# Half as many spare matmuls in the waits of the first batch (75 instead of 148)

## The chip, the core and the metric

The program runs on one NeuronCore of a Trainium2 chip (trn2). The metric is the device time of one execution in microseconds (us). The engines are named as the profile names them: PE is TensorE's matmul stream and PEld its weight loads, DVE is VectorE, ACT is ScalarE, POOL is GpSimd, SP is SyncE, which here issues nearly all DMAs.

## The reference

Everything is float32. An attention with 32 memory slots per head is followed by two wide layers:

```python
def _attn_ref(q, k, v, phi):          # 8 batches, 8 heads, 576 tokens, head width 64
    a = softmax(phi over the tokens)
    k_m = einsum('bhsm,bhsd->bhmd', a, k)
    v_m = einsum('bhsm,bhsd->bhmd', a, v)
    scores = q @ k_m.T / sqrt(64)
    return softmax(scores) @ v_m
x = attention, heads side by side     # 4608 tokens x 512
h = relu(x @ w_in)                    # 2048 wide
x = (s * h * h + b) @ w_out           # 512 wide
h = x @ w1                            # 2048 wide
return (h * sigmoid(1.702 * h)) @ w2  # 512 wide
```

(Shortened; softmax stands for the exponential, the sum with 1e-9 and the division.)

## The kernel before, in words

The kernel describes its work as some thousands of small operations, each with a due time, the tiles it reads and writes and a cost for each engine that could do it. `Order.sort` (L116 on) turns them into one order for each engine by a list of costs; the program is then written out in that order, and every engine runs its own list strictly in that order. Only semaphores hold an engine up.

The work has four stages: the attention with the first layer for eight batches, then the product with `w_out`, with `w1` and with `w2`. This case plays in the first 75 us, in the first batch (b = 0), which is a chain from engine to engine:

1. `slots` (L615 on): the maximum of `phi` over the tokens (two transposes on PE, L638), the exponential (ACT, L653), then 32 small matmuls `s<-kv,ph` (L666) in two halves and 8 more (L672), which need the `kv` tiles from DMA; then the division (DVE, then ACT L688), two transposes (L638) and the copy `km` (ACT L343).
2. `beside` (L723 on): the scores (L753, tile `x`), copied by ACT (L780), transposed (L758, tile `a`), a softmax on DVE and ACT (tile `st`, last step L791), transposed back (L771, tile `y`) and split in a high and a low part, `ah` and `al` (L343, L349). It goes in two parts, 384 columns and 192 columns.
3. `matrix` (L857 on): the weights `wi`, which arrive as float64, two 32-bit words a number, and are converted by ACT, DVE and POOL (`convert`, L378 on), are multiplied by `km` (L871, tile `vw`) and split into `mh` and `ml` (L343, L881, L884).
4. `step` (L887 on): the first layer itself, twelve matmuls a tile `h` (L373 to L375), evicted as `r` (L903, L904) and stored by a DMA `r<-r`.

All inputs come in over one SP queue in a fixed order. The 41 first issues load `phi`, `kv`, `q` and the sixteen `wi` tiles of this batch and the `phi` and `kv` of the next. Behind them stand, in this order, the first store `r<-r`, the next batch's last `kv`, the two scalars `moe_s` and `moe_b` (each broadcast to 128 partitions) and so on; the first tile of `w_out` (`raw<-in_wo`) is the 61st issue. ACT converts that tile (L400) just ahead of the second batch's `km` (L343), which PE needs for that batch's scores (`a<-q,km`, L717).

In the waits of the first batch PE is given spare matmuls: 128 columns of the identity times the identity into a PSUM tile that the next real matmul clears. How many stands in the table `SPARE`, keyed by the tile that the real work opens; `sort` puts the number ahead of the PE operation, and the first use of the tile writes that many. A spare matmul is float32, and PE makes two passes for it, so the trace shows two records for each:

```python
out.append(lambda n=self.SPARE.get(self.opens[n], 0): self.fill and self.fill(n))
...
def idle(self, x, g):
    for _ in range(self.spare):
        self.nc.tensor.matmul(x[:, g, 0:P], self.ident, self.ident, start=True, stop=True)
    self.spare = 0
```

Ten more spare matmuls (`warm`, L1515 on) open the program; they are not in the table.

Of the kernel before, what the change touches and what calls it, by code (L numbers as in the profile page):

```python
# [27 lines left out]
class Order:  # L28
# [7 lines left out]

    SPARE = {
        (('ps', ('s', 0, 0)),): 12,
        (('ps', ('s', 0, 2)),): 15,
        (('ps', ('s', 0, 2)), ('ps', ('s', 0, 2), 1)): 29,  # L40
        (('ps', ('s', 0, 3)),): 10,
        (('ps', ('x', 0, 0)),): 13,
        (('ps', ('vw', 0, 0)),): 8,
        (('ps', ('y', 0, 0)),): 26,
        (('ps', ('h', 0, 0, 0)),): 19,
        (('ps', ('y', 0, 1)),): 4,
        (('ps', ('h', 0, 0, 1)),): 7,
        (('ps', ('s', 1, 0)),): 5,
    }
    FILL, AHEAD, SLACK = 2.5, 120, 0.3  # L50

# [1620 lines left out]
```

## Time and profile before

| what | us |
|---|---|
| median of 3 executions | 1353.36 (1353.16 to 1353.96) |
| the profiled execution | 1354.47 |
| its span, from the first to the last instruction | 1352.7 |
| PE busy in the span | 1344.5 (99%), 9260 passes |
| DVE busy | 1151.1 (85%) |
| ACT busy | 871.4 (64%) |
| POOL busy | 114.8 (8%) |

The profiled execution is 1.1 us above the median and 1.8 us longer than its span. A busy share says how long an engine had an instruction in it, spare matmuls included, so PE's 99% says nothing of what the work was for. The trace can be asked for the instructions of a stretch in order of time, for the waits, for the chain of work that ended last and for the DMAs with the time from their issue to their landing.

### The profile page before, as it was taken

How to read it: one execution, taken by the hardware profiler on the slowest of the kernel's cores; microseconds unless marked ns; L12 is line 12 of the kernel's file. 1: busy time of each engine (PE TensorE's matmuls, PEld its weight loads, DVE VectorE, ACT ScalarE, POOL GpSimd, SP SyncE). 2: the span in 40 equal slices, each digit the busy share in tenths (PEclk: the TensorE clock that was granted, in tenths of full speed). 3: DMA queues.
4: the chain of work that ended last, by engine and by line, in shares of the span. 5: the costliest groups of instructions: out<-in, count | busy, mean ns of one | idle time of the engine just before them, and what ended most of it. 6: DMA issues, size and time to landing. Idle time of an engine off the chain costs nothing.

```text
span 1352.7 us, 24676 instructions
## 1 busy us (share of the span) xinstructions
PE 1344.5 (99%) x9260; PEld 1304.3 (96%) x9260; DVE 1151.1 (85%) x1715; ACT 871.4 (64%) x1230; POOL 114.8 (8%) x112
## 2 busy tenths in 40 slices
PE   9999999999999999999999999999999999999998
PEld 8988888889999999999999999999999999999998
DVE  4778898899999999999998889696375979989995
ACT  3666666698778887898775666565353544645543
POOL 1211231210001000100100000000000001101011
PEclk9999999999999999999999999999999999999999
DMA  9689999897787695898799799879599969779884
GB/s 370 229 307 331 330 354 352 315 339 262 271 270 211 181 311 173 234 320 288 213 343 352 276 360 362 320 270 337 190 372 388 317 204 248 193 235 234 278 245 93
DMA packets 155961, 381.33 MB, mean 282 GB/s; under 512 B 17344, under 2 KB 30528, under 8 KB 155840
## 3 DMA queue, kind: packets, MB, share of 16 engines
q1 hardware_dynamic: 146048, 362.23, 74.8%
q0 software_dynamic: 9792, 17.50, 8.8%
q8 instruction: 73, 1.20, 0.4%
q14 instruction: 48, 0.39, 0.1%
HBM read 226.12 MB, written 153.55 MB: 281 GB/s over the span
## 4 chain that ended last, share of the span: by engine, by line
PE 97%; DMA 2%; ACT 1%; DVE 0%; issue 0%; POOL 0%; POOLq 0%; ACTq 0%; DVEq 0%
PE h L373 5%; PE h L375 5%; PE h L374 5%; PE X L1213 5%; PE X L1212 5%; PE X L1211 5%; PE X L1005 5%; PE X L1007 5%; PE X L1006 5%; PE X L1347 4%; PE X L1348 4%; PE X L1349 4%; PE Y L1007 2%; PE Y L1213 2%; PE Y L1212 2%; PE Y L1006 2%
## 5 line engine op out<-in xcount | busy, mean ns | idle before, releaser
L373 PE MATMUL h<-ah,mh 128*128 128x288 f32 x512 | 156.0, 305 | 0.0
L375 PE MATMUL h<-ah,ml 128*128 128x288 f32 x512 | 150.8, 294 | 0.0
L374 PE MATMUL h<-al,mh 128*128 128x288 f32 x512 | 150.8, 294 | 0.0
L349 DVE TENSOR_TENSOR ol<-A,oh 128x768 fp32r<-128x768 f32 x144 | 136.2, 952 | 13.3 <-ACT oh L343 9.7
L343 ACT CAST oh<-A 128x768 fp32r<-128x768 f32 x126 | 108.4, 869 | 32.2 <-DVE A L349 14.6
L1005 PE MATMUL X<-oh,wo 128*128 128x384 f32 x384 | 128.5, 335 | 0.5 <-ACT u L1031 0.5
L1006 PE MATMUL X<-ol,wo 128*128 128x384 f32 x384 | 128.3, 334 | 0.0
L1007 PE MATMUL X<-oh,wo 128*128 128x384 f32 x384 | 128.3, 334 | 0.0
L1211 PE MATMUL X<-oh,w 128*128 128x384 f32 x384 | 128.3, 334 | 0.0
L1212 PE MATMUL X<-ol,w 128*128 128x384 f32 x384 | 128.3, 334 | 0.0
L1213 PE MATMUL X<-oh,w 128*128 128x384 f32 x384 | 128.3, 334 | 0.0
L903 ACT ACTIVATE r<-h 128x576 f32<-128x576 f32 x126 | 89.0, 708 | 60.7 <-PE h L375 48.1
L373 PEld LDWEIGHTS h<-ah,mh 128*128 128x128 f32 x512 | 96.0, 188 | 17.6 <-issue 10.6
L1347 PE MATMUL X<-oh,w 128*128 128x384 f32 x320 | 107.1, 335 | 0.4 <-ACT u L1366 0.4
L1349 PE MATMUL X<-oh,w 128*128 128x384 f32 x320 | 106.9, 334 | 0.0
L343 ACT CAST oh<-B 128x768 fp32r<-128x768 f32 x88 | 75.4, 874 | 37.7 <-DVE B L349 31.6
L1348 PE MATMUL X<-ol,w 128*128 128x384 f32 x288 | 96.2, 334 | 0.0
L374 PEld LDWEIGHTS h<-al,mh 128*128 128x128 f32 x512 | 96.2, 188 | 0.0
L375 PEld LDWEIGHTS h<-ah,ml 128*128 128x128 f32 x512 | 96.1, 188 | 0.0
L349 DVE TENSOR_TENSOR ol<-B,oh 128x768 fp32r<-128x768 f32 x96 | 89.7, 951 | 6.4 <-ACT oh L343 2.3
L349 DVE TENSOR_TENSOR u<-Y,u 128x768 f32<-128x768 f32 (+1 forms) x50 | 46.8, 937 | 34.8 <-ACT u L1223 22.3
L1005 PEld LDWEIGHTS X<-oh,wo 128*128 128x128 f32 x384 | 72.1, 188 | 0.9 <-ACT u L1031 0.8
(327 smaller groups left out, 3874.9 us busy)
## 6 DMA issues: line engine op xcount, KB each, us to landing
w<-w SPq DMA_DIRECT2D x84, 512.0 KB, 5.8
r<-r SPq DMA_DIRECT2D x128, 288.0 KB, 4.4
kv<-in_kv SPq DMA_DIRECT2D x72, 258.0 KB, 5.4
g<-u SPq DMA_DIRECT2D x48, 384.0 KB, 4.2
raw<-in_w SPq DMA_DIRECT2D x32, 512.0 KB, 6.0
q<-in_q SPq DMA_DIRECT2D x32, 288.0 KB, 5.5
A<-r SPq DMA_DIRECT2D x24, 384.0 KB, 5.4
B<-r SPq DMA_DIRECT2D x24, 384.0 KB, 5.2
```

What stands on the lines that cost most here:

```text
L343: self.order.add(due, [self.act(n, lambda: nc.scalar.copy(out(), src()), psum), self.dve(n, lambda: nc.vector.tensor_copy(out(), src()), f ...
L349: self.order.add(due, [self.dve(n, lambda: nc.vector.tensor_tensor(out(), a(), b(), op=op), port=port)], r, w, first)
L373: self.nc.tensor.matmul(ps, wh, xh, start=start and i == 0, stop=False)
L374: self.nc.tensor.matmul(ps, wh, xl, start=False, stop=False)
L375: self.nc.tensor.matmul(ps, wl, xh, start=False, stop=(i == n - 1))
L1005: nc.tensor.matmul(out, T[w][:, 0, c], T[h][:, p], start=f, stop=False, skip_group_check=True)
L1006: nc.tensor.matmul(out, T[w][:, 0, c], T[l][:, p], start=False, stop=False, skip_group_check=True)
L1007: nc.tensor.matmul(out, T[w][:, 1, c], T[h][:, p], start=False, stop=last, skip_group_check=True)
L1211: nc.tensor.matmul(out, T[w][:, 0, c], T[h][:, k], start=f, stop=False, skip_group_check=True)
L1212: nc.tensor.matmul(out, T[w][:, 0, c], T[l][:, k], start=False, stop=False, skip_group_check=True)
L1213: nc.tensor.matmul(out, T[w][:, 1, c], T[h][:, k], start=False, stop=k == 1, skip_group_check=True)
L1347: nc.tensor.matmul(out, T[w][:, 0, c], T[h][:, p], start=f, stop=False, skip_group_check=True)
```

## The change

Ten of the eleven numbers of the table are lowered; the first stays. The sum goes from 148 to 75.

```diff
     SPARE = {
         (('ps', ('s', 0, 0)),): 12,
-        (('ps', ('s', 0, 2)),): 15,
-        (('ps', ('s', 0, 2)), ('ps', ('s', 0, 2), 1)): 29,
-        (('ps', ('s', 0, 3)),): 10,
-        (('ps', ('x', 0, 0)),): 13,
-        (('ps', ('vw', 0, 0)),): 8,
-        (('ps', ('y', 0, 0)),): 26,
-        (('ps', ('h', 0, 0, 0)),): 19,
-        (('ps', ('y', 0, 1)),): 4,
-        (('ps', ('h', 0, 0, 1)),): 7,
-        (('ps', ('s', 1, 0)),): 5,
+        (('ps', ('s', 0, 2)),): 8,
+        (('ps', ('s', 0, 2)), ('ps', ('s', 0, 2), 1)): 14,
+        (('ps', ('s', 0, 3)),): 4,
+        (('ps', ('x', 0, 0)),): 6,
+        (('ps', ('vw', 0, 0)),): 3,
+        (('ps', ('y', 0, 0)),): 12,
+        (('ps', ('h', 0, 0, 0)),): 9,
+        (('ps', ('y', 0, 1)),): 2,
+        (('ps', ('h', 0, 0, 1)),): 3,
+        (('ps', ('s', 1, 0)),): 2,
     }
```

The order of all other instructions is the same on every engine. On PE, around the second part of the first batch's softmax, the program before reads as follows (`y` is the PSUM tile of the transposed softmax `st`, `h` that of the first layer, `ident` the identity; the number behind a name counts the instructions written before it):

```order
L758 MATMUL a_376<-ident,sc_320 128x128 x2
L758 MATMUL a_376<-ident,sc_324 128x128 x2
L307 MATMUL y_404<-ident 128x128 x26
L771 MATMUL y_404<-ident,st_373 128x128 x6
L881 MATMUL vw_353<-mh_396,less 128x512 x2
L307 MATMUL h_468<-ident 128x128 x19
L373 MATMUL h_468<-ah_445,mh_396 128x288
```

The same place in the program of the change:

```order
L758 MATMUL a_336<-ident,sc_285 128x128 x2
L758 MATMUL a_336<-ident,sc_289 128x128 x2
L307 MATMUL y_364<-ident 128x128 x12
L771 MATMUL y_364<-ident,st_333 128x128 x6
L881 MATMUL vw_318<-mh_356,less 128x512 x2
L307 MATMUL h_414<-ident 128x128 x9
L373 MATMUL h_414<-ah_391,mh_356 128x288
```

Only the two rows of L307 differ, 26 to 12 and 19 to 9; the numbers behind the names fall because fewer instructions stand ahead.

## Rows read from the trace of the kernel before

**Rows 1.** Page, part 4: the chain that ended last, by engine.
```profile
PE 97%; DMA 2%; ACT 1%; DVE 0%; issue 0%; POOL 0%; POOLq 0%; ACTq 0%; DVEq 0%
```

**Rows 2.** PE's waits, whole execution, longest after the start: total us, times, longest us.
```profile
PE Z L1460 <- ACT z L1478: 0.9, 1, 0.9
```

**Rows 3.** Timeline of PE, 0 to 75 us: start us, us, engine, line, op, tiles, passes.
```profile
1.36 4.63 PE L307 MATMUL warm<-ident 128*128 128x128 f32 x20 [1.36 <-POOL ident masks.py:199]
...
13.14 1.12 PE L666 MATMUL s<-kv,ph 128*32 128x129 f32 x32
...
20.86 1.12 PE L666 MATMUL s<-kv,ph 128*32 128x129 f32 x32
...
24.66 0.38 PE L638 MATMUL s<-ident,an 128*128 128x128 f32 x2
...
27.88 1.20 PE L753 MATMUL x<-q,km 64*32 64x384 f32 x32
...
33.55 5.97 PE L307 MATMUL y<-ident 128*128 128x128 f32 x52
39.36 0.82 PE L771 MATMUL y<-ident,st 128*128 128x128 f32 x6
...
45.26 0.29 PE L374 MATMUL h<-al,mh 128*128 128x288 f32 x1
...
47.20 0.60 PE L771 MATMUL y<-ident,st 128*128 128x128 f32 x4
...
57.26 0.29 PE L375 MATMUL h<-ah,ml 128*128 128x288 f32 x1
...
72.89 1.20 PE L717 MATMUL a<-q,km 64*32 64x288 f32 x32
```

**Rows 4.** Timelines of ACT and DVE, 0 to 75 us: the data that PE's spares precede.
```profile
10.76 1.47 ACT L653 ACTIVATE ph<-ph 128x640 f32<-128x640 f32 x2 [3.71 <-DVE ph L650]
...
22.96 0.63 ACT L688 ACTIVATE an<-s,nm 128x128 f32<-128x128 f32 x2 [5.51 <-DVE nm L681]
...
35.09 0.96 DVE L791 TENSOR_TENSOR st<-st,a 128x768 f32<-128x768 f32 x1
...
42.40 0.55 DVE L349 TENSOR_TENSOR al<-y,ah 128x384 fp32r<-128x384 f32 x1
...
44.50 0.68 DVE L791 TENSOR_TENSOR st<-st,a 128x512 f32<-128x512 f32 x1
...
55.97 1.00 ACT L884 CAST ml<-vw 128x1024 fp32r<-128x1024 f32 x1
```

**Rows 5.** DMA issues of 8.8 to 8.9 us: xcount, KB each, us to landing.
```profile
kv<-in_kv SPq DMA_DIRECT2D x1, 258.0 KB, 6.1
```

**Rows 6.** DMA issues of 38.0 to 38.1 us, the last before a pause.
```profile
kv<-in_kv SPq DMA_DIRECT2D x1, 258.0 KB, 5.3
```

**Rows 7.** Windows: length, busy us of PE, PEld, DVE, ACT, POOL, PEclk, DMA share, GB/s.
```profile
43.50:50.90 7.40, 7.40 (x64) 7.40 (x63) 5.39 (x13) 5.60 (x12) 1.40 (x1) 1.00 0.01 2
60.00:80.00 20.00, 19.99 (x266) 15.18 (x265) 15.68 (x27) 12.01 (x18) 6.07 (x5) 1.00 1.05 403
```

**Rows 8.** DMA issues of 50.9 to 51.0 us, the first behind the pause.
```profile
r<-r SPq DMA_DIRECT2D x1, 288.0 KB, 2.1
```

**Rows 9.** DMA issues of 51.3 to 52.6 us, one row each.
```profile
kv<-in_kv SPq DMA_DIRECT2D x1, 258.0 KB, 2.9
sc<-in_moe_s SPq DMA_DIRECT2D x1, 0.5 KB, 4.3
sc<-in_moe_b SPq DMA_DIRECT2D x1, 0.5 KB, 6.1
```

**Rows 10.** DMA issues of 64.6 to 64.7 us.
```profile
raw<-in_wo SPq DMA_DIRECT2D x1, 512.0 KB, 6.3
```

**Rows 11.** Timeline of ACT, 69 to 73 us.
```profile
71.06 0.70 ACT L400 ACTIVATE raw<-raw 128x512 uint32<-128x512 uint32 x1 [0.54 <-DMA raw<-in_wo]
71.66 0.35 ACT L343 COPY km<-s 128x256 f32<-128x256 f32 x1
```

## Prediction

> **What bounds the kernel now.** I read the chain of work that ended last first: 97% of it is PE [rows 1]. Then PE's waits over the whole execution: apart from the start, the longest is 0.9 us [rows 2]. So from the first matmul on PE is hardly ever seen idle, and time that PE gains early can only be lost again where PE would have to wait for something that does not move with it. The question is then what PE was busy with. In the first 57 us a part of it is spare matmuls, which no one needs. The timeline of PE shows when each real instruction behind a run of spares began [rows 3]; the timelines of ACT and DVE and the DMA views show when the data that it needs were there [rows 4 to 6]. The reader is to see that the second time lies well before the first at nearly every place: the spares last longer than the waits that they fill. A spare is two passes, and 52 passes ahead of the tile `y` last from 33.55 to 39.36 us [rows 3], 0.112 us a pass, 0.224 us a spare.
>
> **What the change removes.** 73 spares, 146 passes at 0.112 us: 16.3 us of PE's time, all of it in the first 57 us. It adds nothing and moves nothing else: each of the other engines and the DMA queue has the list it had. What each run of spares gives is the smaller of two numbers. One is PE's lead so far plus the passes taken out. The other is the lead of what the data come from, plus the slack, which is the time from the data being there to the start of the real instruction. I go through the runs that decide, in order.
>
> - First half of `s<-kv,ph`, 14 passes out, 1.6 us. It waits for the first of two exponentials, which ends near 11.5 us (half of the pair [rows 4]); PE started at 13.14 [rows 3], slack 1.6. Lead 1.6 us.
> - Second half, 30 passes out, 3.4 us. Its last `kv` tile was issued at 8.8 us and landed 6.1 us later, at 14.9 [rows 5]; PE started at 20.86 [rows 3]. That load does not move, but the slack is 5.9 us, so PE gets all of its 1.6 + 3.3. Lead 4.9 us.
> - The transposes of `an`, 12 out, 1.3 us. ACT ended the second `an` at 23.59 [rows 4]; the second transpose starts 0.11 us after the row's 24.66 [rows 3], slack 1.2, and `an` comes from the step before: 4.9 + 1.2 = 6.1, against 4.9 + 1.3 = 6.2. Lead 6.1 us.
> - The scores at 27.88 [rows 3], 14 out, 1.6 us. Nothing near limits them: lead 7.7 us.
> - `vw`, 10 out, and `y`, 28 out: together 4.3 us. The softmax `st` ends at 36.05 [rows 4], `y` starts at 39.36 [rows 3], slack 3.3. `st` comes from the scores, 7.7 + 3.3 = 11.0; PE alone would have 12.0. Lead 11.0 us; a new wait of up to a microsecond, in one or two pieces, is what is left of the difference.
> - First `h`, 20 out, 2.2 us. The last split `al` ends at 42.95 [rows 4], its matmul starts at 45.26 [rows 3], slack 2.3 and a lead of 11.0 for its source: PE's 13.2 is the smaller. Lead 13.2 us.
> - Second `y`, 4 out, 0.4 us. `st` ends at 45.18 [rows 4], PE starts at 47.20 [rows 3], slack 2.0: 11.0 + 2.0 = 13.0. Lead 13.0 us.
> - The last two runs, 14 out, 1.6 us. `ml` ends at 56.97 [rows 4] and its matmul starts at 57.26 [rows 3], slack 0.3: of the 1.6 us at most 0.3 stays. Lead 13.0 to 13.3, say 13.2 us, at 57 us.
>
> So of 16.3 us some 13.2 come out as lead, and 3.1 us come back as short waits, each below 1 us: there ACT, DVE and POOL are the chain.
>
> **What does not move with PE.** The DMA queue. Its first 41 loads depend on nothing that PE does; the last was issued at 38.0 us and landed 5.3 us later, at 43.3 [rows 6]. Then comes a pause, with a DMA share of 0.01 [rows 7], because the next issue, the store `r<-r`, waits for the first result. It was issued at 50.9 and landed at 53.0 [rows 8]; its 288 KB at the 403 GB/s of the full queue [rows 7] are 0.7 us, so its data began to move at 52.3. Behind it the next `kv` landed at 51.35 + 2.9 = 54.25 [rows 9], 1.2 us after the store, of which 0.7 are its own: 0.5 us more of pause. From there to 80 us the queue is full, share 1.05 [rows 7]. With PE 13 us ahead the store is ready at about 38 us, so the pause goes. The queue can gain no more than this pause: 52.3 - 43.3 = 9.0, and 0.5, less rounding: 9.4 us.
>
> That matters in one place. The first `w_out` tile, issued at 64.67, landed at 71.0 [rows 10]. ACT waited for it, 0.54 us, converted it and only then copied the second batch's `km`, until 72.01 [rows 11]. PE's next scores start at 72.89 [rows 3], slack 0.9. In the changed kernel the tile lands 9.4 us earlier, `km` is there at 62.6, and PE, which would arrive at 72.9 - 13.2 = 59.7, waits some 2.9 us: that is what is late next. Lead 9.4 + 0.9 = 10.3 us.
>
> **The sum.** 16.3 removed, 3.1 back in short waits, 2.9 back behind the full queue: 10.3 us. Later I find nothing that takes more: the waits of PE are short throughout [rows 2], and the other engines are fed by PE and move with it. Against the profiled execution, 1354.47 us, that is 1344.2; this execution is 1.1 us above the median, 1353.36, so I forecast 1343.1.
>
> The price that the trace of before does not show is how the queue takes the change. Above, the store, `kv` and what is behind them fill the pause without loss: lead 10.3. At best the queue holds PE up nowhere: 13.2, and 1340.2. This would happen if the two loads of the scalars, half a KB each, which landed at 56.1 and 58.4 [rows 9], 1.9 and 2.3 us apart where 288 KB take 0.7, cost less when the queue is full. At worst the transfers of the 18 us from 53.0 to 71.0 run 10% slower for it, 1.8 us: lead 8.5. I take the middle one, as it is made of the rows themselves.
>
> **A rule against the change.** The spares are there for the clock. The granted clock is 1.00 in both windows [rows 7], with PE busy throughout. The first 20 passes took 4.63 us [rows 3], 0.22 us each where later ones take 0.112, so the array works at 1.2 GHz before it has worked for a while, and at 2.4 GHz after. The Trainium skill, "TensorE: Matmul & The Clock Gate", section "HAM oscillation", says that waits between bursts of matmuls put the array back to the half clock and that each burst then begins slow. By that rule the new waits would cost what rival 3 below works out. The trace of before has no such wait in which to see it.
>
> **Rivals.** I call a difference of 0.2%, 2.7 us, about what a measurement of this kernel can tell from no change.
>
> 1. *The forecast*, the lead cut to 10.3 us by the queue: 1343.1. Chance 0.52.
> 2. *The queue does not cut it.* Lead 13.2, 1340.2. For it: the two scalars' loads move almost nothing, and 2.9 us less in the 18 us behind the pause is enough. Against: other loads landed behind them in order. Chance 0.17.
> 3. *The clock falls once*, most likely in the wait of 2.9 us before L717. Then the next stretch runs slow until the clock is back. It took 4.4 us of work at the half clock to rise at the start [rows 3], which is 2.2 us lost: lead 8.1, 1345.3. For it: the wait is three times as long as any now. Chance 0.13.
> 4. *The fuller queue costs more*, 1.8 us as above, or holds up another load that has no slack: 1344 to 1346. For it: the stretch at share 1.05 [rows 7]. Chance 0.09.
> 5. *The spares cover waits that the trace does not show*, so that the real instructions start where they did and the change does nothing: 1353.4. Against: PE went from spares into real work without a pause everywhere, and data were there 1 to 6 us before [rows 3, 4, 5]; where spares end too early a pause would show. Chance 0.05.
> 6. *Slower: the clock falls in the first waits and stays low while the matmuls come in short groups.* From the first `h` to 72.89 PE has 28 us of work, 3.6 of them spares (32 passes). At half the clock 24.7 us are added, against a lead of 13.2: 1365. It decides when more than 13.2 us of real work runs at 1.2 GHz. Against: 4.4 us of dense work brought the clock up at the start [rows 3], the new waits are short and half the spares stay. Chance 0.04.
>
> **How the numbers follow.** The likeliest case gives 1343.1. Cases 1 to 4 make 0.91; their ends are 1340.2 less 0.7 for the size of my slacks, and 1343.1 with both losses of cases 3 and 4, 2.2 + 1.8, at 1347.1. I give 1339.5 to 1347.5, which holds a little over 8 in 10. All four are faster by over 0.2%: 0.91. Case 5 is no change: 0.05. Case 6 is slower: 0.04.
>
> **What would show it right or wrong.** In the changed profile the second half of `s<-kv,ph` begins near 16 us, `y` near 28.4, the first `h` near 31.5, and the second batch's scores near 62.6, with PE waiting 2 to 3 us for ACT's `km` just before and ACT waiting for `raw<-in_wo`. The DMA share between 43 and 51 us is near 1. The granted clock stays 1.00. After the scores all of PE lies 10.3 us earlier to the end. If L717 begins near 59.7 case 2 is right; if the matmuls behind it come at twice their interval, case 3. I am wrong altogether if the real instructions behind the spares begin where they did, or if the lead is there at 75 us and gone at the end.

## The result and the profile after

The changed kernel takes 1339.82 us in the median of 4 executions (1338.62 to 1343.35) against 1353.26 us, in the same round, for the kernel before: 13.4 us less, a ratio of 0.9904 with a 95% interval of 0.9885 to 0.9924. A second round of both gave 1338.92 against 1352.35 us, 0.9905 (0.9887 to 0.9922). One of the eight executions of the kernel before in that round took 1461.95 us at a granted clock of 0.85 and is left out. The time is inside the range of the forecast, 0.3 us above its lower end, and faster, as forecast; but it lies at case 2 (1340.2), not at the case that I took for the likeliest (1343.1). The profiled execution took 1340.30 us, its span is 1338.5.

The timeline of PE of the changed kernel, the lines that answer to [rows 3] (start us, us, engine, line, op, tiles, passes, and in brackets the idle time before and what ended it):

```profile
9.13 0.38 PE L638 MATMUL s<-ident,am 128*128 128x128 f32 x2
...
12.18 1.12 PE L666 MATMUL s<-kv,ph 128*32 128x129 f32 x32
...
16.55 1.12 PE L666 MATMUL s<-kv,ph 128*32 128x129 f32 x32
...
19.07 0.59 PE L638 MATMUL s<-ident,an 128*128 128x128 f32 x2
...
20.92 1.20 PE L753 MATMUL x<-q,km 64*32 64x384 f32 x32
...
26.21 2.84 PE L307 MATMUL y<-ident 128*128 128x128 f32 x24
29.14 0.87 PE L771 MATMUL y<-ident,st 128*128 128x128 f32 x6
...
32.87 0.37 PE L374 MATMUL h<-al,mh 128*128 128x288 f32 x1
...
35.07 0.66 PE L771 MATMUL y<-ident,st 128*128 128x128 f32 x4 [0.46 <-DVE st L791]
...
44.46 0.40 PE L375 MATMUL h<-ah,ml 128*128 128x288 f32 x1
...
60.20 1.20 PE L717 MATMUL a<-q,km 64*32 64x288 f32 x32
```

Each starts earlier than its line in [rows 3]: by 1.0, 4.3, 5.6, 7.0, 10.2, 12.4, 12.1, 12.8 and, for the second batch's scores, 12.7 us. The first line shown begins 0.6 us later than in the execution of before (8.53), since here the opening passes stayed at the slow interval for longer: the 24 passes just ahead of it took 3.50 us, for 2.90 before. That is no part of the change; with it taken out the leads are 1.6, 4.9, 6.2, 7.6, 10.8, 13.0, 12.7, 13.4 and 13.3 us, where the forecast had 1.6, 4.9, 6.1, 7.7, 11.0, 13.2, 13.0 and 13.2, and then 10.3 for the last.

So the new wait before L717 did not come. The timeline of ACT around the second batch's `km`, for [rows 11]:

```profile
58.30 0.68 ACT L400 ACTIVATE raw<-raw 128x512 uint32<-128x512 uint32 x1 [0.47 <-POOL wi L467]
58.88 0.35 ACT L343 COPY km<-s 128x256 f32<-128x256 f32 x1
```

Before, what ended ACT's wait was the DMA of the `w_out` tile; now it is POOL, and `km` is done at 59.23, 0.97 us before L717 needs it. It was closer than this one profile shows. The same two rows of e0, the changed kernel once more:

```profile
59.06 0.67 ACT L400 ACTIVATE raw<-raw 128x512 uint32<-128x512 uint32 x1 [1.41 <-DMA raw<-in_wo]
59.64 0.35 ACT L343 COPY km<-s 128x256 f32<-128x256 f32 x1
```

There ACT does wait for the tile, and `km` is done at 59.99, 0.05 us before L717 begins at 60.04; the step from `km` to L717 is as short in e7 below, where PE does wait for it. So in e0 the queue only just held nothing up. The DMA views of the changed kernel say why the tile is in time, first the issues of 40.2 to 40.5 and 40.9 to 41.1 us (the two scalars), then that of 51.95 to 52.0 us (the `w_out` tile), for [rows 9, 10]; columns: xcount, KB each, us from issue to landing.

```profile
sc<-in_moe_s SPq DMA_DIRECT2D x1, 0.5 KB, 4.8
...
sc<-in_moe_b SPq DMA_DIRECT2D x1, 0.5 KB, 4.3
...
raw<-in_wo SPq DMA_DIRECT2D x1, 512.0 KB, 6.2
```

The scalars were issued at 40.32 and 40.98 and land at 45.10 and 45.27, 0.2 us apart, where they were 2.3 us apart in [rows 9]. The tile lands at 58.2 instead of 71.0: 12.8 us earlier, not 9.4. The pause itself is gone, as forecast. The windows of 43.5 to 50.9 and of 38 to 60 us (length, busy us of PE, PEld, DVE, ACT, POOL, granted clock, DMA share, GB/s), for [rows 7]:

```profile
43.50:50.90 7.40, 7.24 (x76) 5.81 (x78) 6.71 (x12) 3.79 (x6) 1.64 (x1) 1.00 0.96 359
38.00:60.00 22.00, 21.80 (x234) 18.41 (x233) 18.81 (x30) 14.16 (x23) 10.17 (x7) 1.00 0.99 370
```

The DMA share went from 0.01 to 0.96, and the granted clock stayed at 1.00. PE's busy time of the whole execution fell from 1344.5 to 1330.3 us, the passes from 9260 to 9114, by the 146 removed; DVE, ACT and POOL are busy as long as before, within 1.0 us.

### The profile page after: what moved, and what is told of

Its sections match the earlier page's. It is cut to its first block, busy times and chain, and to the rows that moved or that the text cites. A ratio compares the mean times of both kernels' runs of the same rounds, so it can differ in the third digit from the quotient of the medians.

```text
span 1338.5 us, 24384 instructions
## 1 busy us (share of the span) xinstructions
PE 1330.3 (99%) x9114; PEld 1289.3 (96%) x9114; DVE 1151.1 (86%) x1715; ACT 870.4 (65%) x1230; POOL 114.9 (9%) x112
## 4 chain that ended last, share of the span: by engine, by line
PE 53%; DVE 1%; ACT 0%; issue 0%; DVEq 0%; ACTq 0%
PE X L1212 5%; PE X L1213 5%; PE X L1211 5%; PE X L1347 4%; PE X L1348 4%; PE X L1349 4%; PE Y L1347 2%; PE Y L1348 2%; PE Y L1212 2%; PE Y L1213 2%; PE Y L1349 2%; PE Y L1211 2%; PE Z L1461 2%; PE Z L1460 2%; PE Z L1462 2%; PE Z L1282 1%
## 5 line engine op out<-in xcount | busy, mean ns | idle before, releaser
L1005 PE MATMUL X<-oh,wo 128*128 128x384 f32 x384 | 128.6, 335 | 1.8 <-ACT u L1031 1.8
L1005 PEld LDWEIGHTS X<-oh,wo 128*128 128x128 f32 x384 | 72.1, 188 | 2.6 <-ACT u L1031 2.6
```

The lines of the kernel that those rows point to most:

```text
L1005: nc.tensor.matmul(out, T[w][:, 0, c], T[h][:, p], start=f, stop=False, skip_group_check=True)
```

## The experiments

**The two parts alone, and the whole once more.** If the lead is really the smaller of two numbers at each run of spares, each part of the table has a size of its own that can be worked out beforehand. e0 is the changed kernel again; e1 takes the first two of its numbers, e2 the other eight:

```diff
 e1, against the kernel before
-        (('ps', ('s', 0, 2)),): 15,
-        (('ps', ('s', 0, 2)), ('ps', ('s', 0, 2), 1)): 29,
+        (('ps', ('s', 0, 2)),): 8,
+        (('ps', ('s', 0, 2)), ('ps', ('s', 0, 2), 1)): 14,
 e2, against the changed kernel
-        (('ps', ('s', 0, 2)),): 8,
-        (('ps', ('s', 0, 2)), ('ps', ('s', 0, 2), 1)): 14,
+        (('ps', ('s', 0, 2)),): 15,
+        (('ps', ('s', 0, 2)), ('ps', ('s', 0, 2), 1)): 29,
```

Expected of e0: 

> The changed kernel once more, as the base for its neighbours of this round. Expected as in its first profile: the second batch's scores (L717) begin within 0.7 us of 60.2, the whole is 13 to 14 us faster than before.

Expected of e1: 

> The first two lowered numbers alone (15 to 8, 29 to 14), all others as before. Theory 'smaller of two numbers' (PE's lead plus passes taken out, or the data's lead plus slack): 44 passes give 4.9 us of lead at the second half of the kv product, and every later run keeps its spares, so the lead stays 4.9: L717 near 68.0, total 4.9 us faster. Rival 'the later data are bound by loads that do not move': the lead shrinks behind the first half, total 0 to 3 us faster.

Expected of e2: 

> The other eight lowered numbers alone; 15 and 29 as before. Same theory: 102 passes are 11.4 us, of which the slack of each run (1.2, 3.1, 3.3, 2.3, 2.0) lets through 8.2 us: L717 near 64.7, total 8.2 us faster, and together with the first part 13.1. Rival 'one long chain': most of the gain needs both parts, and each alone gives less than its share, with a sum well below 13.

Measured, against 1352.35 us for the kernel before in this round: e0 1338.92 us, 0.9905 (0.9887 to 0.9922); e1 1347.27 us, 0.9963 (0.9949 to 0.9976); e2 1343.26 us, 0.9930 (0.9912 to 0.9947). That is 13.4, 5.1 and 9.1 us less by the medians. The start of the second batch's scores says it with less noise. The first fence below is of e0's timeline of PE, the next of e1's, the last of e2's:

```profile
8.58 0.38 PE L638 MATMUL s<-ident,am 128*128 128x128 f32 x2
...
60.04 1.20 PE L717 MATMUL a<-q,km 64*32 64x288 f32 x32
```

```profile
8.91 0.38 PE L638 MATMUL s<-ident,am 128*128 128x128 f32 x2
...
16.58 1.12 PE L666 MATMUL s<-kv,ph 128*32 128x129 f32 x32 [0.18 <-DMA kv<-in_kv]
...
68.61 1.20 PE L717 MATMUL a<-q,km 64*32 64x288 f32 x32
```

```profile
7.79 0.38 PE L638 MATMUL s<-ident,am 128*128 128x128 f32 x2
...
63.77 1.20 PE L717 MATMUL a<-q,km 64*32 64x288 f32 x32
```

From the first transposes to L717 it takes 64.36 us before (72.89 [rows 3] less 8.53), and 51.46, 59.70 and 55.98 us in e0, e1 and e2: leads of 12.9, 4.7 and 8.4 us, for 13.1, 4.9 and 8.2 expected. The parts add up to 13.0. Neither rival holds: the gain of the first part is still there behind loads that do not move, and neither part needs the other. The line of e1 at 16.58 sets a limit to the forecast's slack of 5.9 us at this place: PE waits 0.18 us for the `kv` tile, which landed at 16.45 here and at 14.9 in [rows 5]. In the nine profiles it landed anywhere between these two times, so this slack is that of one execution, and with half of the spares as little as nothing is left of it.

**No spares at all, and a quarter.** If the data set the pace, fewer spares still must give nothing more. Then it shows what the remaining ones are for.

```diff
 e3, against the changed kernel (the first number, 12, stays in both)
-        8, 14, 4, 6, 3, 12, 9, 2, 3, 2
+        0, 0, 0, 0, 0, 0, 0, 0, 0, 0
 e8, against the changed kernel
-        8, 14, 4, 6, 3, 12, 9, 2, 3, 2
+        4, 7, 2, 3, 1, 6, 4, 1, 1, 1
```

Expected of e3: 

> No spares at all in the ten runs (only the 12 of the first and the opening ten stay). If the data set the pace and the clock stays up: waits of PE appear in place of the spares (up to 3 us before the tile y), the lead at L717 is the same as with half of them, about 13.1 us, total within 1 us of the changed kernel. If the clock falls in these waits, matmuls behind them come at twice their interval, the granted clock shows a low stretch before 50 us, and it is slower than the changed kernel by 2 us or more.

Expected of e8: 

> A quarter of the spares: 12, then 4, 7, 2, 3, 1, 6, 4, 1, 1, 1 (42 in all). The data set the pace, so if the clock stays up the lead at L717 is again 13.1 us and the time that of the changed kernel within 1 us. If the clock falls as it did without spares, a stretch of half clock shows between 10 and 40 us and 1 to 3 us are lost.

Measured: e3 1340.40 us, 0.9912 (0.9896 to 0.9928); e8 1339.77 us against 1353.92 us in its round, 0.9902 (0.9887 to 0.9917). As whole times neither can be told from the changed kernel's 0.9904. For e3 that is a miss in part: I had expected 2 us or more if the clock fell, and the medians of e3 and e0 differ by 1.5 us, within the spread of e0's four executions (1337.90 to 1342.33). The profiles can be told apart. The windows of e3 (columns as above; the last but two is the granted clock):

```profile
12.40:25.90 13.50, 8.87 (x108) 4.35 (x104) 9.76 (x17) 7.11 (x15) 2.98 (x2) 0.50 1.04 404
26.10:29.30 3.20, 0.95 (x10) 0.42 (x4) 3.06 (x7) 3.13 (x5) 0.00 (x0) 1.00 1.03 410
29.50:39.60 10.10, 9.31 (x32) 7.56 (x33) 8.47 (x17) 8.61 (x18) 1.29 (x1) 0.50 1.03 398
40.00:60.00 20.00, 19.56 (x216) 15.94 (x215) 18.66 (x30) 12.82 (x20) 8.68 (x6) 1.00 0.87 324
```

For some 24 of the 30 us from 10 to 40 us the granted clock is 0.50, 1.2 GHz instead of 2.4. Its timeline of PE has the waits in and before these stretches:

```profile
11.36 1.13 PE L666 MATMUL s<-kv,ph 128*32 128x129 f32 x32 [1.68 <-ACT ph L653]
15.66 1.96 PE L666 MATMUL s<-kv,ph 128*32 128x129 f32 x32 [3.17 <-DMA kv<-in_kv]
...
20.43 2.17 PE L753 MATMUL x<-q,km 64*32 64x384 f32 x32 [0.46 <-ACT km L343]
...
30.01 1.51 PE L771 MATMUL y<-ident,st 128*128 128x128 f32 x6 [2.96 <-DVE st L791]
...
62.38 1.20 PE L717 MATMUL a<-q,km 64*32 64x288 f32 x32
```

The 32 passes of `s<-kv,ph` take 1.96 us and those of the scores 2.17, for 1.12 and 1.20 at the full clock. L717 begins at 62.38, 54.03 us behind the first transposes at 8.35: a lead of 10.3, 2.6 us below e0's. So without spares the clock falls, and L717 comes 2.6 us later; no wait of PE stands before L717 itself. PE is busy for 18.2 of the 23.6 slow us, and at nearly twice the time a pass the slow matmuls cost far more than 2.6 us of it; I read the rest as time that PE would have spent waiting for data, which no run separated. The Trainium skill ("TensorE: Matmul & The Clock Gate", "HAM oscillation") has this rule, that bursts with waits between them begin at the half clock. For the bursts behind the waits of 3.17 and 2.96 us this trace agrees; the one behind the wait of 1.68 us took 1.13 us, which is the full clock. The length of a wait is not all that counts: by 12.40 us the granted clock is 0.50, and the wait of 3.17 us begins only when that burst ends, at 12.49.

In e8 the granted clock is 1.00 in both of these windows, and L717 is where the changed kernel has it:

```profile
10.00:40.00 30.00, 23.27 (x253) 17.43 (x259) 25.51 (x45) 22.66 (x43) 5.95 (x4) 1.00 1.03 402
40.00:60.00 20.00, 19.57 (x218) 16.38 (x204) 17.02 (x27) 11.64 (x18) 9.12 (x6) 1.00 1.00 351
```

```profile
60.35 1.20 PE L717 MATMUL a<-q,km 64*32 64x288 f32 x32
```

With 8.47 us for its first transposes that is 51.88 us, a lead of 12.5. PE is idle for 6.7 of the 30 us, spread over more and shorter waits (its longest is 1.6 us, before `y`), and loses at most 0.4 us by it. From 75 spares on down nothing is to be gained, as expected; somewhere between 42 and 12 in all they are too few to keep the clock up.

**The queue.** The forecast charged the queue for the two scalars. e6 is the kernel before with these two loads moved into the stretch where the queue is full; e7 is the changed kernel with the queue made longer again, by five copies of `q` tiles, 288 KB each, into memory that nothing reads:

```diff
 e6, against the kernel before
-            self.dma(10, lambda i=i: self.sc[:, i:i + 1], lambda x=x: ..., (), (("sc", 0, i),), 1)
+            self.dma(-30, lambda i=i: self.sc[:, i:i + 1], lambda x=x: ..., (), (("sc", 0, i),), 1)
 e7, against the changed kernel
+        for i in range(5):
+            self.dma(10, lambda i=i: self.dram("fill", i, cols=self.S), lambda i=i: self.a["q"][1 + i // 4, i % 4], (), (("fill", i),), 1)
```

Expected of e6: 

> The kernel before, spares as before, with the two scalar loads (moe_s, moe_b) moved forward in the SP queue to where it is full (behind about 25 issues). Theory 'a scalar load costs the queue 1.9 to 2.3 us only behind a pause': in the full queue each lands about 0.2 us after its neighbour, and without them behind the pause the q loads land near 55 us instead of 59, the first w_out tile near 68 instead of 71.0. Theory of the forecast 'they cost 4.1 us wherever they stand': everything behind them in the full queue lands 4 us later, kv included. Time: PE has 0.9 us of slack at L717 and is held by the spares, so within 1 us of the kernel before by the first theory.

Expected of e7: 

> The changed kernel with five extra loads of 288 KB (into memory that nothing reads) behind the two scalars: 5 x 0.73 us = 3.65 us of queue, about what the forecast had charged for the scalars. If the way of the forecast's cut is right (w_out tile, then ACT's conversion, then km, then L717), the tile lands near 61.9 instead of 58.2, ACT waits for it, L717 begins near 62.9 instead of 60.2, and the loss of 2.7 us stays to the end: about 10.6 us faster than before, 2.7 us behind the changed kernel. Rival 'the queue has slack enough': L717 stays at 60.2 and the time is that of the changed kernel.

Measured, e6: 1353.16 us against 1353.92, 0.9997 (0.9987 to 1.0007), no change, as expected of a kernel whose PE is held by spares. The DMA views of e6, issues of 19.2 to 20.1 us (the scalars) and of 63.5 to 63.6 us (the `w_out` tile), and its timeline of ACT:

```profile
sc<-in_moe_s SPq DMA_DIRECT2D x1, 0.5 KB, 7.8
...
sc<-in_moe_b SPq DMA_DIRECT2D x1, 0.5 KB, 8.5
```

```profile
raw<-in_wo SPq DMA_DIRECT2D x1, 512.0 KB, 5.0
```

```profile
69.73 0.68 ACT L400 ACTIVATE raw<-raw 128x512 uint32<-128x512 uint32 x1
70.72 0.38 ACT L343 COPY km<-s 128x256 f32<-128x256 f32 x1 [0.31 <-PE s L638]
```

The tile landed at 68.6, 2.4 us earlier than in [rows 10], and ACT no longer waits for it. Not all of the 2.4 us come from the edit: in this execution the first transposes began 0.7 us earlier (7.86), and so the store that ends the pause landed 0.6 us earlier. From that store to the tile it takes 16.1 us, for 18.0 with the scalars in between: 1.9 us less, and not 4.1, since a `q` tile behind the pause landed 1.65 us after its neighbour now, and other loads after it came late too. In the full queue the scalars landed 0.5 and 1.4 us behind their neighbours, where I had expected 0.2 each; with their 1.9 in all they cost less than half of the 4.1 us behind the pause, but not nothing.

The profiles of e1, e2 and e3 hold the same two loads, and they speak against the pause as the one reason. First e2, issues of 43.2 to 43.9 us, then e3, 41.8 to 42.5 us:

```profile
sc<-in_moe_s SPq DMA_DIRECT2D x1, 0.5 KB, 4.9
sc<-in_moe_b SPq DMA_DIRECT2D x1, 0.5 KB, 5.8
```

```profile
sc<-in_moe_s SPq DMA_DIRECT2D x1, 0.5 KB, 3.2
sc<-in_moe_b SPq DMA_DIRECT2D x1, 0.5 KB, 5.3
```

They landed 2.0 and 1.9 us behind their neighbours in e1, 2.65 and 1.4 in e2, 0.2 and 2.5 in e3. In e2 hardly any pause was left (the store landed 0.9 us behind the last load), and still they took 4.0 us. In the four profiles in which they took 0.2 to 0.3 us each (the changed kernel, e0, e7, e8) each was issued 4 us or more before the load ahead of it landed; in the kernel before, e1, e2 and e3 the first was issued 2.3 to 3.0 us before. But e6, where it was 7 us, shows that this is not all that sets the price.

Measured, e7: 1344.31 us against 1353.92, 0.9939 (0.9923 to 0.9956), behind the changed kernel's 0.9904. The way of the cut is the one that the forecast described. From e7's timelines of ACT and of PE:

```profile
62.83 0.65 ACT L400 ACTIVATE raw<-raw 128x512 uint32<-128x512 uint32 x1 [4.90 <-DMA raw<-in_wo]
63.39 0.35 ACT L343 COPY km<-s 128x256 f32<-128x256 f32 x1
```

```profile
63.79 2.17 PE L717 MATMUL a<-q,km 64*32 64x288 f32 x32 [3.45 <-ACT km L343]
65.72 1.81 PE L871 MATMUL vw<-wi,km 64*32 64x512 f32 x16
67.45 0.40 PE L373 MATMUL h<-ah,mh 128*128 128x288 f32 x1
```

ACT waits for the tile, PE for `km`, and L717 begins 3.6 us later than in the changed kernel; 2.7 were expected, but the extra loads took 0.9 us each, not 0.73. By the medians e7 is 9.6 us faster than the kernel before, for 10.6 expected. What I had not written into this expectation is the second loss. The windows of e7:

```profile
60.30:63.70 3.40, 0.05 (x1) 0.00 (x0) 0.00 (x0) 0.87 (x3) 0.00 (x0) 1.00 1.04 403
63.90:67.20 3.30, 3.30 (x48) 1.01 (x48) 1.58 (x4) 1.00 (x2) 0.00 (x0) 0.50 1.06 405
67.30:75.00 7.70, 7.70 (x79) 5.80 (x72) 6.94 (x14) 6.66 (x9) 0.00 (x0) 1.00 0.74 290
```

Behind this one long wait the clock is at 0.50 for some 3.4 us. From L717 to the next `h` it takes 3.66 us, for 1.99 in the kernel before (72.89 to 74.88 in its timeline): 1.7 us more. This is case 3 of the forecast, at a price near the 2.2 us given there, and it needed the wait of case 1 first. The wait and the slow stretch are 5.1 us in this profile; the medians show some 4 of them (9.6 us of gain for 13.4).

## Why the forecast was right, and where it was not

- *What the change removes.* 73 spares, 146 passes at 0.112 us, 16.3 us: the pass count fell by 146, and the leads follow the passes taken out wherever the data allowed it. Right.
- *The smaller of two numbers at each run.* Right at every place of the first batch, within 0.3 us (corrected for the different start), and in e1 and e2 for tables that the trace of before had never shown. 3.1 us were to come back as short waits. The changed kernel's lead of 13.3 us at L717 out of 16.3 is that.
- *What does not move with PE: the DMA queue.* That it is the next thing to come late, and by which way, was right: e7 shows the chain from the tile to L717. The step that failed is "The queue can gain no more than this pause". It gained 12.8 us at the `w_out` tile, 3.4 more than the 9.4 forecast, because the two scalars took 0.3 us of the queue and not 4.1. I had taken the 1.9 and 2.3 us between their landings for their time in the queue; [rows 9] show them behind a pause, and e6 and the changed kernel show less than half of it, or next to nothing, where the queue has work ahead of them. The rest of the queue moved little: from the first store to the tile it took 17.95 us before and 13.94 now, which without the scalars' 4.15 and 0.34 is 13.8 and 13.6 (14.4 in e0), so of the 1.8 us of case 4 at most 0.6 came. So the term of 2.9 us in the sum was zero, in e0 with nothing to spare: 16.3 less 3.1, 13.2 us, for 13.4 measured. I had named this as the condition of case 2 and gave it 0.17. That the range held the time is owed to its having been drawn to take in case 2, and not to the path that I thought the likeliest.
- *A rule against the change, and case 3.* The clock stayed up in the changed kernel, where no wait of PE in this stretch is longer than 0.52 us, and in e8, where the longest is 1.64 us. With no spares (e3, waits of up to 3.17 us) or with one wait of 3.45 us (e7) it fell. So the fall that was feared does come in this kernel, and half of the spares, or a quarter, still kept it away.
- *Later stages.* "Later I find nothing that takes more": the leads at L717 (12.7 and 12.9 us in the two profiles) are there at the end, where the spans differ by 14.2 and 15.0 us. On the way the first profile of the changed kernel loses 1.4 us again, at a wait of PE of 1.3 us at 499 us (tile `X`, L1005, for ACT) that the profile of before has not. The rest came in short waits of PE late in the program that are in the profile of before and smaller or absent in these two: the one of [rows 2] is absent and 0.7 us, and one of 0.8 us at L1461, for DVE's `ol`, is absent in both. e6, which has the spares of before, lacks the second too, and its profiled execution is 1.3 us shorter, 0.7 of it by its earlier start; so I take this for the spread of single executions, not for the change.
- *Case 5 and 6.* The real instructions moved, and nothing ran slow: both fell. One argument against case 6 did not hold in e3: 4.4 us of dense work had brought the clock up at the start, but from 29.5 to 39.6 us it stayed at 0.50 with PE busy for 9.3 of these 10.1 us.

Open is what a scalar's load costs exactly and what sets it: 0.2 us behind large loads in the changed kernel, 0.5 and 1.4 us in e6, 1.9 and 2.3 behind the pause, 2.65 and 1.4 in e2 with hardly a pause. No run separated the issue from the transfer. Open too is why two of the eight executions of the changed kernel took 1342.3 and 1343.4 us where the others are within 1337.9 to 1340.3; neither was profiled.

## What to carry to other kernels

Work that fills a wait has to be measured in the trace: compare the time at which the waited-for data are there with the time at which the real instruction begins, and take out what lies between. The gain of a series of such places is a running minimum, of the engine's lead plus what was removed, and of the data's lead plus the slack; it can be summed by hand. A price read where a queue has just stood still need not be the price of the same transfer at another place: the same two loads took between 0.3 and 4.1 us here.

## What the runs showed of the hardware

- Two loads of 0.5 KB, each spread to 128 partitions, landed 1.9 and 2.3 us behind the load ahead of them when they were issued shortly behind a pause (the kernel before), 2.65 and 1.4 us with hardly a pause (e2), 0.5 and 1.4 us amid loads of 512 KB (e6), and 0.2 us each when some 4 us of transfers stood ahead of them (the changed kernel).
- At 1.2 GHz the 32 small passes of L717 take 2.17 us (e7), for 1.20 at 2.4 GHz.
- The opening stretch at the slow interval is not equally long in all executions: the same first transposes begin between 7.79 (e2) and 9.13 us (the changed kernel) with the same instructions ahead of them. This moves PE's work behind it, by more than some of the effects that were looked for.
